# Retention attention and squared-ReLU FFN on one core: attention on 64-wide PE tiles, hand-fixed engine orders, weights by column slices

## Chip, cores, metric

One core of a Trainium2 chip. The metric is device time in microseconds (us) of that core, lower is better. Every ratio compares a kernel with the kernel before on the same chip in the same rounds. PE is the tensor engine, DVE the vector engine, ACT the scalar engine, POOL the GpSimd engine, SP the engine that issues the DMAs; SPq is SP's own queue of instructions, PEld are PE's weight loads, PSUM is the memory that PE writes to. In profile lines L288 is line 288 of the kernel, hp and op are the outputs of the FFN's first and second layer, tp a chunk's transposes, st its scores, yt its y, c the carry into the state. The span is the time from the first to the last instruction of the profiled execution.

## The reference, cut

```python
# q, k, v: (4, 8, 768, 64) float32; 8 heads, gamma[h] = 1 - 2**(-5-h)
for t in range(S):
    state = gamma * state + k[t] (x) v[t]          # (64 x 64) for each head
    y[t] = scale * q[t] @ state
# x = y as (3072 tokens, 512)
h = maximum(x @ w_in, 0)                           # w_in  (512, 2048)
out = (h * h) @ w_out                              # w_out (2048, 512), out (3072, 512)
```

The kernels work in chunks of 128 tokens, 24 in all, six to a sequence. In a chunk, scores k·q are masked and multiplied with v, and what earlier chunks left is added through a state. The FFN works on blocks of chunks: a first layer of 16 groups of 4 matmuls, then a second layer of 16 matmuls of 512 columns for each chunk.

## The kernel before

A scheduler orders the instructions. Parts (`...` marks cuts):

```python
# order of loads: chunks 0 to 3, all of w_in, all of w_out, then chunk 4 and on
if not w_in_issued and t + 2 == (chunks_per_blk[0] - 1):
    while w_in_q:  w_in_q.pop(0)()       # 4 rows of blocks, 1 MB each
    while w_out_q: w_out_q.pop(0)()      # 4 x 1 MB
...
def stage_b(m, s_prev):                  # y = v^T p + s^T q, 128 columns wide
    for hh in range(2):
        ytile = ps_yt.tile([P, 4, P], FP32, tag=f"yt{hh}")
        for p in range(4):
            nc.tensor.matmul(ytile[:, p, :], lhsT=vs[:, 2*p:2*p+2, :], rhs=pt[:, 2*p+hh, :], ...)
            if i > 0:
                nc.tensor.matmul(ytile[:, p, :], lhsT=s_prev[:, p, :], rhs=qT[:, p, :], ...)
        nc.scalar.activation(xt[rows, 0:4, off:off+C], ytile[rows, :, :], AF.Copy)   # half is used
    ...                                   # 4 matmuls for the carry, add, two memsets
...
def ffn_steps(tb):                        # blocks of 512 tokens
    for fb in range(NFB):
        ...                               # 4 matmuls of 512 columns, relu on ACT, square on DVE
        yield
    if tb == 0:
        cast_w_out()                      # after block 0's whole first layer
    for q4 in range(TB // 128):
        ...                               # 16 matmuls of 512 columns, copy, store
        yield
```

Of the kernel before, what the change touches and what calls it, by code (L numbers as in the profile page):

```python
# [18 lines left out]
def kernel(  # L20
# [14 lines left out]
    NTOK = B * S  # L35
    assert D == 64 and H == 8 and DM == H * D
    C = 128
    assert S % C == 0
    NCH = S // C
    if NTOK % 512 == 0:  # L40
        blk_sizes = [512] * (NTOK // 512)
    else:
        blk_sizes = [NTOK]
    assert sum(blk_sizes) == NTOK
    blk_starts = [int(sum(blk_sizes[:i])) for i in range(len(blk_sizes))]
    TBMAX = max(blk_sizes)
    NTB = len(blk_sizes)
    NFB = DFF // 128
    NCB = DM // 128
    assert NFB * 128 == DFF  # L50
    scale = 1.0 / float(np.sqrt(D))
    gammas = [1.0 - 2.0 ** (-5.0 - h) for h in range(H)]

    const = ctx.enter_context(tc.tile_pool(name="const", bufs=1))
    xtpool = ctx.enter_context(tc.tile_pool(name="xtpool", bufs=1))
    ldpool = ctx.enter_context(tc.tile_pool(name="ldpool", bufs=3))
    work = ctx.enter_context(tc.tile_pool(name="work", bufs=2))
    qkvpool = ctx.enter_context(tc.tile_pool(name="qkvpool", bufs=3))
    qktpool = ctx.enter_context(tc.tile_pool(name="qktpool", bufs=3))
    spool = ctx.enter_context(tc.tile_pool(name="spool", bufs=2))  # L60
    hpool = ctx.enter_context(tc.tile_pool(name="hpool", bufs=1))
    wstage = ctx.enter_context(tc.tile_pool(name="wstage", bufs=1))
    opool = ctx.enter_context(tc.tile_pool(name="opool", bufs=3))
    ps_tp = ctx.enter_context(tc.tile_pool(name="ps_tp", bufs=1, space=bass.MemoryType.PSUM))
    ps_st = ctx.enter_context(tc.tile_pool(name="ps_st", bufs=1, space=bass.MemoryType.PSUM))
    ps_yt = ctx.enter_context(tc.tile_pool(name="ps_yt", bufs=1, space=bass.MemoryType.PSUM))
    ps_c = ctx.enter_context(tc.tile_pool(name="ps_c", bufs=1, space=bass.MemoryType.PSUM))
    ps_f = ctx.enter_context(tc.tile_pool(name="ps_f", bufs=2, space=bass.MemoryType.PSUM))
# [11 lines left out]
    )  # L80
    cmask = const.tile([P, P], BF16)
# [10 lines left out]
    lng = const.tile([P, H], FP32)  # L92
    for h in range(H):
        nc.gpsimd.memset(lng[:, h : h + 1], float(np.log(gammas[h])))
    ex_i = const.tile([P, NCH, H], I32)
    nc.gpsimd.iota(
        ex_i[:], pattern=[[C, NCH], [0, H]], base=0, channel_multiplier=1
    )
# [8 lines left out]
    qf = const.tile([P, NCH, H], FP32)  # L107
    nc.scalar.activation(qf[:], ex_f[:], AF.Exp)
    nc.vector.tensor_scalar_mul(qf[:], qf[:], scale)
    kf = const.tile([P, NCH, H], FP32)  # L110
    nc.scalar.activation(kf[:], ex_f[:], AF.Exp, scale=-1.0)

    w_in_bf = const.tile([P, NCB, DFF], BF16)
    w_out_bf = const.tile([P, NFB, DM], BF16)
    w_in_f = wstage.tile([P, NCB, DFF], FP32)
    w_out_f = wstage.tile([P, NFB, DM], FP32)
    w_in_v = moe_w_in.rearrange("(cb p) f -> p cb f", p=P)
    w_out_v = moe_w_out.rearrange("(fb p) n -> p fb n", p=P)

    w_in_q = [  # L120
        (lambda cb=cb: nc.sync.dma_start(w_in_f[:, cb, :], w_in_v[:, cb, :]))  # L121
        for cb in range(NCB)
    ]
    w_out_q = []
    per = min(4, NFB)
    for fb0 in range(0, NFB, per):
        n = min(per, NFB - fb0)
        w_out_q.append(
            lambda fb0=fb0, n=n: nc.sync.dma_start(
                w_out_f[:, fb0 : fb0 + n, :], w_out_v[:, fb0 : fb0 + n, :]  # L130
            )
        )

    def flush_w_out():
        while w_out_q:
            w_out_q.pop(0)()

    def cast_w_in():
        for cb in range(NCB):
            if cb % 2 == 0:  # L140
                nc.vector.tensor_copy(w_in_bf[:, cb, :], w_in_f[:, cb, :])
            else:
                nc.scalar.activation(w_in_bf[:, cb, :], w_in_f[:, cb, :], AF.Copy)  # L143

    def cast_w_out():
        for fb in range(NFB):
            if fb % 2 == 0:
                nc.vector.tensor_copy(w_out_bf[:, fb, :], w_out_f[:, fb, :])
            else:
                nc.scalar.activation(w_out_bf[:, fb, :], w_out_f[:, fb, :], AF.Copy)  # L150

    xts = [
        xtpool.tile([P, NCB, blk_sizes[tb]], BF16, name=f"xt{tb}")
        for tb in range(NTB)
    ]

    def token_block(tok0):
        for tb in range(NTB):
            if blk_starts[tb] <= tok0 < blk_starts[tb] + blk_sizes[tb]:
                return tb  # L160
        raise ValueError(tok0)

    actx: dict = {}

    def stage_a0(m):
        b, i = chunk_batches[m]
        qn = ldpool.tile([P, H, D], FP32)
        nc.sync.dma_start(qn[:], q[b, :, i * C : (i + 1) * C, :].rearrange("h s d -> s h d"))
        kn = ldpool.tile([P, H, D], FP32)
        nc.sync.dma_start(kn[:], k[b, :, i * C : (i + 1) * C, :].rearrange("h s d -> s h d"))  # L170
        vn = ldpool.tile([P, H, D], FP32)
        nc.sync.dma_start(vn[:], v[b, :, i * C : (i + 1) * C, :].rearrange("h s d -> s h d"))

        qs = qkvpool.tile([P, H, D], BF16)
        nc.vector.tensor_tensor(  # L175
            out=qs[:],
            in0=qn[:],
            in1=qf[:, i, :, None].to_broadcast([P, H, D]),
            op=ALU.mult,
        )  # L180
        ks = qkvpool.tile([P, H, D], BF16)
        nc.vector.tensor_tensor(  # L182
            out=ks[:],
            in0=kn[:],
            in1=kf[:, i, :, None].to_broadcast([P, H, D]),
            op=ALU.mult,
        )
        vs = qkvpool.tile([P, H, D], BF16)
        nc.vector.tensor_copy(vs[:], vn[:])

        tp = ps_tp.tile([P, H, P], BF16)
        for p in range(4):
            nc.tensor.transpose(tp[:, p, :], qs[:, 2 * p : 2 * p + 2, :], ident[:])  # L193
        for p in range(4):
            nc.tensor.transpose(tp[:, 4 + p, :], ks[:, 2 * p : 2 * p + 2, :], ident[:])  # L195
        qkT = qktpool.tile([P, H, P], BF16)
        nc.scalar.activation(qkT[:], tp[:], AF.Copy)  # L197
        actx[m] = dict(qs=qs, ks=ks, vs=vs, qkT=qkT)

    def stage_a1(m):  # L200
        cm = actx[m]
        qkT = cm["qkT"]
        qT = qkT[:, 0:4, :]
        kT = qkT[:, 4:8, :]
        st_ps = ps_st.tile([P, 2, 4, P], FP32)
        for p in range(4):
            for hh in range(2):
                rows = slice(64 * hh, 64 * (hh + 1))
                nc.tensor.matmul(  # L209
                    st_ps[:, hh, p, :],  # L210
                    lhsT=kT[rows, p, :],
                    rhs=qT[rows, p, :],
                    start=True,
                    stop=True,
                )
        pt = work.tile([P, H, P], BF16)
        pt_v = pt.rearrange("s (p hh) t -> s hh p t", hh=2)
        nc.vector.tensor_tensor(  # L218
            out=pt_v,
            in0=st_ps[:],  # L220
            in1=cmask[:, None, None, :].to_broadcast([P, 2, 4, P]),
            op=ALU.mult,
        )
        cm["pt"] = pt

    def stage_b(m, s_prev):
        b, i = chunk_batches[m]
        cm = actx.pop(m)
        ks, vs, pt = cm["ks"], cm["vs"], cm["pt"]
        qT = cm["qkT"][:, 0:4, :]  # L230
        tok0 = b * S + i * C
        tb = token_block(tok0)
        off = tok0 - blk_starts[tb]
        xt = xts[tb]

        for hh in range(2):
            ytile = ps_yt.tile([P, 4, P], FP32, tag=f"yt{hh}")
            for p in range(4):
                h = 2 * p + hh
                nc.tensor.matmul(  # L240
                    ytile[:, p, :],
                    lhsT=vs[:, 2 * p : 2 * p + 2, :],
                    rhs=pt[:, h, :],
                    start=True,
                    stop=(i == 0),
                )
                if i > 0:
                    assert s_prev is not None
                    nc.tensor.matmul(  # L249
                        ytile[:, p, :],  # L250
                        lhsT=s_prev[:, p, :],
                        rhs=qT[:, p, :],
                        start=False,
                        stop=True,
                    )
# [5 lines left out]
        if i == NCH - 1:  # L261
            return None
# [68 lines left out]
    for t in range(-2, NCHUNK):  # L331
# [8 lines left out]
        if 0 <= t + 1 < NCHUNK:  # L340
            stage_a1(t + 1)
# [58 lines left out]
```

## Time and profile before

| | before |
|---|---|
| time | 246.35 us (2 runs, 246.2 to 246.5) |
| PE busy | 223.1 of 246.7 us, 90% |
| share of the chain that ended last | FFN matmuls hp 33% and op 32% |
| w_in in the chain | 15.2 us of DMA |

These are rows of the profile page of the kernel before: busy tenths in 40 equal slices (6.2 us each), the granted clock of PE in tenths, the busy tenths of the DMA engines, and GB/s.

```profile
PE   0395459999999999999999999999999999999994
...
PEclk9999558999999999999999999999999999999999
DMA  6999996998535999389698714100220001210022
GB/s 139 226 265 409 379 390 172 229 187 191 143 86 126 197 230 176 85 213 213 137 178 170 200 58 116 43 4 7 78 89 0 0 3 43 85 43 3 2 83 85
```

PE is dense from the seventh slice on. Nearly all that can be won without less work is in the first six. The first rows of GB/s also give two rates: q, k and v come in rows of 256 bytes at about 220 GB/s, the weights at 380 to 410.

The chain that ended last, from 15.9 us (columns: start, duration, what):

```profile
15.94 15.17 DMA w_in_f<-in_moe_w_in_dram
...
31.13 1.92 ACT w_in_bf L143
...
34.39 14.29 PE hp L288 x53
```

The first steady FFN matmul starts at 34.39 us, after the last part of w_in has landed and been cast.

PE in time in the steady part: start, duration from first start to last end, tile, shape, count. A duration holds the latency of the last matmul, so the cost of a group is the distance to the next start.

```profile
110.67 1.03 PE L288 MATMUL hp<-xt_135,w_in_bf 128*128 128x512 bf16 x4
111.53 0.39 PE L193 MATMUL tp<-ident,qs 128*128 128x128 bf16 x4
111.75 0.39 PE L195 MATMUL tp<-ident,ks 128*128 128x128 bf16 x4
112.07 0.40 PE L209 MATMUL st_ps<-qkT 64*128 64x128 bf16 x8
112.40 0.62 PE L240 MATMUL ytile<-pt,vs 128*128 128x128 bf16 x8
112.86 0.39 PE L265 MATMUL c_ps<-vs,ks 128*128 128x128 bf16 x4
113.08 4.67 PE L288 MATMUL hp<-xt_135,w_in_bf 128*128 128x512 bf16 x20
```

This chunk begins a sequence, so eight state matmuls are missing. Four full matmuls take 0.22 us (0.055 each). From the second transposes to the scores it is 0.32 us, 0.10 more: the change to 64-row tiles. Two lines of the chain mark a whole block (64 + 64 FFN matmuls and four chunks of attention), 35.37 us:

```profile
110.83 0.86 PE hp L288 x4
...
146.20 0.86 PE hp L288 x4
```

### The profile page before, as it was taken

To read this page: it belongs to the slowest core of one execution; us is meant where nothing else is said; L and a number is where in the kernel's file an instruction comes from. 1 tells how busy PE (TensorE), PEld (TensorE's weight loads), DVE (VectorE), ACT (ScalarE), POOL (GpSimd) and SP (SyncE) were. 2 spreads that over 40 slices of the span, in tenths; PEclk is the share of its full clock that TensorE was granted. 3 is DMA by queue.
4 is the path that set the end of the run, shared out by engine and by line. 5 is a ranking of instruction groups with operands and counts; after the bars stand their busy time and mean duration, and the time that the engine had idled before them with its cause. 6 is when DMAs were issued, how large, how long until landed. Compare 5 with 4: busy or idle time off the path is not lost.

```text
span 246.7 us, 3969 instructions
## 1 busy us (share of the span) xinstructions
PE 223.1 (90%) x1584; PEld 117.6 (48%) x1584; DVE 122.5 (50%) x225; ACT 129.8 (53%) x205; POOL 14.1 (6%) x57
## 2 busy tenths in 40 slices
PE   0395459999999999999999999999999999999994
PEld 0374013455555555445655455555465554444441
DVE  0797125775766888117888018674037630044200
ACT  2256376945637877118775137883158661176210
POOL 2001000000100010000000001000000000000000
PEclk9999558999999999999999999999999999999999
DMA  6999996998535999389698714100220001210022
GB/s 139 226 265 409 379 390 172 229 187 191 143 86 126 197 230 176 85 213 213 137 178 170 200 58 116 43 4 7 78 89 0 0 3 43 85 43 3 2 83 85
DMA packets 81042, 33.81 MB, mean 137 GB/s; under 512 B 75392, under 2 KB 75392, under 8 KB 80512
## 3 DMA queue, kind: packets, MB, share of 16 engines
q1 hardware_dynamic: 81024, 33.56, 55.0%
q8 instruction: 12, 0.20, 0.4%
q14 instruction: 6, 0.05, 0.1%
HBM read 27.26 MB, written 6.29 MB: 136 GB/s over the span
## 4 chain that ended last, share of the span: by engine, by line
PE 78%; DMA 8%; ACT 8%; SPq 2%; DVE 2%; issue 1%; ACTq 0%
PE hp L288 33%; PE op L304 32%; DMA w_in_f<-in_moe_w_in_dram 6%; ACT qkT L197 4%; PE ytile L240 3%; PE ytile L249 3%; PE st_ps L209 3%; DMA vn<-in_v_dram 2%; PE tp L193 2%; PE tp L195 2%; PE c_ps L265 1%; ACT xt_134 L257 1%; SPq L121 1%; ACT w_in_bf L143 1%; DVE qs L175 1%
## 5 line engine op out<-in xcount | busy, mean ns | idle before, releaser
L288 PEld LDWEIGHTS <-w_in_bf 128*128 128x128 bf16 x384 | 36.9, 99 | 51.9 <-issue 6.7
L312 ACT ACTIVATE osb<-op 128x512 f32<-128x512 f32 x24 | 14.3, 598 | 58.4 <-PE op L304 55.7
L218 DVE TENSOR_TENSOR pt<-st_ps,cmask 128x1024 bf16<-128x1024 f32 x24 | 29.3, 1220 | 5.4 <-PE st_ps L209 5.0
L197 ACT ACTIVATE qkT<-tp 128x1024 bf16<-128x1024 bf16 x24 | 24.5, 1021 | 12.3 <-PE tp L195 11.4
L175 DVE TENSOR_TENSOR qs<-qn,qf 128x512 bf16<-128x512 f32 x24 | 16.4, 686 | 21.2 <-PE tp L193 12.3
L240 PE MATMUL ytile<-pt,vs 128*128 128x128 bf16 x192 | 24.2, 224 | 1.6 <-DVE pt L218 1.3
L288 PE MATMUL hp<-xt_133,w_in_bf 128*128 128x512 bf16 x64 | 19.2, 446 | 6.0 <-ACT w_in_bf L143 4.1
L249 PE MATMUL ytile<-qkT,s_new 128*128 128x128 bf16 x160 | 21.1, 220 | 0.0
L240 PEld LDWEIGHTS <-vs 128*128 128x128 bf16 x192 | 17.6, 100 | 2.8 <-issue 0.4
L296 DVE TENSOR_TENSOR h_2576<-h_2576 128x512 bf16<-128x512 bf16 x16 | 6.8, 425 | 21.7 <-ACT h_2576 L295 21.7
L277 POOL MEMSET s_new<- 64x256 bf16 x20 | 6.5, 326 | 182.6 <-DVE s_new L276 132.7
L249 PEld LDWEIGHTS <-s_new 128*128 128x128 bf16 x160 | 15.7, 98 | 2.5 <-POOL s_new L278 1.3
L182 DVE TENSOR_TENSOR ks<-kn,kf 128x512 bf16<-128x512 f32 x24 | 16.4, 685 | 0.5 <-DMA kn<-in_k_dram 0.5
L265 PE MATMUL c_ps<-vs,ks 128*128 128x128 bf16 x80 | 8.4, 232 | 8.9 <-DVE ks L182 8.9
L296 DVE TENSOR_TENSOR h_2197<-h_2197 128x512 bf16<-128x512 bf16 x16 | 6.8, 424 | 19.4 <-ACT h_2197 L295 19.4
L304 PE MATMUL op<-w_out_bf,h_452 128*128 128x512 bf16 x64 | 16.3, 380 | 0.0
L288 PE MATMUL hp<-xt_134,w_in_bf 128*128 128x512 bf16 x64 | 15.8, 379 | 0.1
L288 PE MATMUL hp<-xt_136,w_in_bf 128*128 128x512 bf16 x64 | 14.6, 379 | 0.1
L288 PE MATMUL hp<-xt_135,w_in_bf 128*128 128x512 bf16 x64 | 14.6, 379 | 0.0
L288 PE MATMUL hp<-xt_137,w_in_bf 128*128 128x512 bf16 x64 | 14.5, 379 | 0.0
L288 PE MATMUL hp<-xt_138,w_in_bf 128*128 128x512 bf16 x64 | 14.0, 379 | 0.0
L304 PE MATMUL op<-w_out_bf,h_1332 128*128 128x512 bf16 x64 | 14.0, 379 | 0.0
(57 smaller groups left out, 310.5 us busy)
## 6 DMA issues: line engine op xcount, KB each, us to landing
qn<-in_q_dram SPq DMA_DIRECT2D x24, 256.0 KB, 4.8
kn<-in_k_dram SPq DMA_DIRECT2D x24, 256.0 KB, 4.4
vn<-in_v_dram SPq DMA_DIRECT2D x24, 256.0 KB, 4.7
out_dram<-osb SPq DMA_DIRECT2D x24, 256.0 KB, 2.1
w_in_f<-in_moe_w_in_dram SPq DMA_DIRECT2D x4, 1024.0 KB, 12.0
w_out_f<-in_moe_w_out_dram SPq DMA_DIRECT2D x4, 1024.0 KB, 17.8
```

The source lines that it names most:

```text
L175: nc.vector.tensor_tensor(out=qs[:], in0=qn[:], in1=qf[:, i, :, None].to_broadcast([P, H, D]), op=ALU.mult,)
L182: nc.vector.tensor_tensor(out=ks[:], in0=kn[:], in1=kf[:, i, :, None].to_broadcast([P, H, D]), op=ALU.mult,)
L197: nc.scalar.activation(qkT[:], tp[:], AF.Copy)
L209: nc.tensor.matmul(st_ps[:, hh, p, :], lhsT=kT[rows, p, :], rhs=qT[rows, p, :], start=True, stop=True,)
L218: nc.vector.tensor_tensor(out=pt_v, in0=st_ps[:], in1=cmask[:, None, None, :].to_broadcast([P, 2, 4, P]), op=ALU.mult,)
L240: nc.tensor.matmul(ytile[:, p, :], lhsT=vs[:, 2 * p : 2 * p + 2, :], rhs=pt[:, h, :], start=True, stop=(i == 0),)
L249: nc.tensor.matmul(ytile[:, p, :], lhsT=s_prev[:, p, :], rhs=qT[:, p, :], start=False, stop=True,)
L265: nc.tensor.matmul(c_ps[:, p, :], lhsT=ks[:, 2 * p : 2 * p + 2, :], rhs=vs[:, 2 * p : 2 * p + 2, :], start=True, stop=True,)
L288: nc.tensor.matmul(hp[:, :TB], lhsT=w_in_bf[:, cb, fb * 128 : (fb + 1) * 128], rhs=xt[:, cb, :], start=(cb == 0), stop=(cb == NCB - 1),)
L296: nc.vector.tensor_mul(h2[:, fb, :TB], h2[:, fb, :TB], h2[:, fb, :TB])
L304: nc.tensor.matmul(op[:], lhsT=h2[:, fb, q4 * 128 : (q4 + 1) * 128], rhs=w_out_bf[:, fb, :], start=(fb == 0), stop=(fb == NFB - 1),)
L312: nc.scalar.activation(osb[:], op[:], AF.Copy)
```

## The change

The intent: y and the carry on 64-wide tiles of PE, two at a time, in place of 128-wide matmuls of which half is thrown away; the state summed in PSUM over a sequence and the decay applied when y is read out, which takes copies and memsets away; the order of each engine's instructions fixed by hand; two first blocks of 256 tokens and w_in by column slices, so that the FFN can start when a quarter of w_in is there.

The diff, cut to its core:

```diff
+    blocks = [[0, 1], [2, 3]]                       # then blocks of 4 chunks
+    ctx.enter_context(tc.manual_schedule())
...
+    for m in range(4):
+        load_chunk(m)
+    for s in range(NSL):
+        load_w("i", s)                              # column slices of w_in, 1 MB each
...
-                nc.tensor.matmul(ytile[:, p, :], lhsT=vs[:, 2*p:2*p+2, :], rhs=pt[:, h, :], ...)
-                    nc.tensor.matmul(ytile[:, p, :], lhsT=s_prev[:, p, :], rhs=qT[:, p, :], ...)
+                    nc.tensor.matmul(yt[r, p, :], lhsT=s_bf[r, p, :], rhs=kqT[r, 1, p, :], ...)   # 64x64
+                nc.tensor.matmul(yt[r, p, :], lhsT=vs[:, 2*p+hh, :], rhs=pt[:, hh, p, :], ...)    # 128x64
+                    nc.tensor.matmul(c[r, p, :], lhsT=ks[:, h, :], rhs=vs[:, h, :], ...)          # 128x64
...
+    load_chunk(4)
+    load_w("o", 0)
+    load_chunk(5)
+    load_w("o", 1)
+    load_chunk(6)
+    load_w("o", 2)
+    load_chunk(7)
+    load_w("o", 3)
+    load_chunk(8)
...
+    q1 = all_f1(1)                                  # block 1's first layer, 16 groups
+    for x in range(NFB // 2):
+        q1[x]()
+        if x % 2 == 0:
+            cast_w("o", x // 2)                     # half on DVE, half on ACT
+    weave(q1[NFB // 2 :] + all_f2(0) + all_f2(1), stages(blocks[2]))
```

`stages` lists the attention steps of a block (for each chunk: scores of the chunk before, its three casts, its transposes, the output of the chunk two before), and `weave` spreads them between FFN steps. Casts of w_out stand in ACT's and DVE's fixed order, so the relu of block 1's eighth group stands behind the cast of the last slice.

## The prediction

> What bounds the kernel now. The engine table gives PE 223 of 246.7 us (90%). The chain of waits holds 65% in the FFN matmuls (hp, op); their 768 matmuls of 512 columns start 0.216 us apart (64 in 13.8 us), so 166 us of the span cannot go. From 45 us on the windows table shows PE busy almost without a gap. The loss is at the start: the first steady FFN matmul comes at 34.4 us, after w_in's casts, which wait for w_in's DMA (chain: 15.2 us); by then PE has done only 4 of 24 chunks of attention and 8 FFN matmuls, and the granted clock is 0.5 until about 38 us. The DMA slices show 256-byte q/k/v traffic saturating at about 220 GB/s (3.6 us a chunk) and weights at about 395 GB/s (2.65 us a MB).
>
> What the change does to PE in steady state. A middle chunk took about 2.0 us: 8 transposes 0.44, 8 scores 0.33, 16 y matmuls 0.9, 4 state matmuls 0.22. The 64-row scores start 28 ns apart, full ones 55 ns, so two tiles do run together; estimated from that, y falls to 16 x 28 ns = 0.45 and the state stays near 0.2. But the scores cost about 0.1 us of gap on each side in the timeline. The Trainium skill ("TensorEngine Tiling (Array Packing)", Key Properties) says changing the tiling mode drains the engine; the trace agrees (0.10 and 0.12 us). The new order has about five switches a chunk in place of two. It also says (Restrictions) that column tiling disables fast weight load; no run shows that yet. I estimate 1.75 us a chunk, so about 4 us saved over 20 chunks, not 10. Copies removed on ACT (1.2 us a chunk), POOL memsets and lighter DVE work are off the critical path.
>
> What it does to the start. Two blocks of 256 tokens and w_in column slices let FFN begin near 22 us instead of 25 to 34. But w_out's four slices are now queued behind chunks 4 to 7, and their casts stand in ACT's and DVE's order inside block 1's first FFN layer: the relu of its eighth group comes after the cast of the last slice. Bytes before that slice: 8.39 MB of weights and 6.29 MB of q/k/v. At the measured rates: 2.2 + 21.2 + 28.6 = 52 us, plus lag and cast, about 54 us. Until then PE can do only 4 chunks of attention, block 0's first layer and ten groups of block 1: a hole of some 20 us, mostly from 32 to 54. At 54 us the old kernel has done 89 FFN matmuls and 6 chunks; the new one 52 equivalents and 4.
>
> Sum: 54 + 716 x 0.216 (155) + 20 x 1.75 (35) + slow clock after the hole 2 + tail 3.6 + in-order stalls 3 to 5 (cast to turn on DVE: 1.5 us cast, 1.2 us mask) = about 253 us.
>
> Predicted 253 us, range 245 to 261. Faster by over 2%: 7%; within 2%: 35%; slower by over 2%: 58%.
>
> What would show it: last w_out slice landing at 50 to 56 us; PE tenths near 1 to 3 between 32 and 54 us, with waits ending in the w_out casts on ACT/DVE; steady FFN from about 55 us; a chunk's attention at 1.5 to 2.0 us of PE with gaps of 0.1 us at each mode switch; the y multiply off the chain; PE dense afterwards.
>
> What would make it wrong: DMA delivering the mix faster, so that the hole closes by 45 us; mode switches that cost nothing and pairs truly at 28 ns (attention 1.3 us, 8 us less); or column tiles loading weights serially at over 50 ns each (6 to 8 us more), or stalls in DVE's fixed order at every chunk.

## The result, and the profile after

| | before | after |
|---|---|---|
| time | 246.35 us | 260.36 us (2 runs, 259.56 and 261.15) |
| ratio, 95% interval | | 1.0585 (1.048 to 1.069) |
| PE busy | 223.1 us | 219.8 us |
| PE at work with no gap over 1 us from | 34 us | 60 us |

A ratio is the mean time of one kernel's fast runs over that of the other's of the same rounds, so it is not quite the ratio of the medians. Four more runs of the changed kernel later (after_again, below) gave 260.45 us and a ratio of 1.0619.

The same rows of the page, after (slices of 6.5 us):

```profile
PE   1546674207899999999999999999999999999994
...
PEclk9999998555999999999999999999999999999999
DMA  7999889981011398021992124971119601210022
GB/s 175 246 316 397 218 213 271 278 246 33 0 43 54 97 261 200 0 82 43 217 246 64 40 77 114 247 175 39 44 47 252 149 0 43 81 43 0 0 81 81
```

PE works more than before in slices one, two and four to six, and then there is a hole: 4, 2, 0 in the slices from 39 to 58 us, in which the clock falls to a half. The DMA rate in slices five to nine is 213 to 278 GB/s, though weights are among the bytes.

The chain that ended last, through the hole:

```profile
38.75 4.21 SPq L81
...
43.08 0.78 SPq L92
...
45.25 4.13 SPq L81
...
49.49 7.71 DMA wo_368<-in_moe_w_out_dram
...
57.23 1.06 ACT w_out_bf_176 L166
58.28 0.28 ACT h_1_563 L299
...
58.59 0.29 DVE h_1_563 L300
58.88 0.61 DVE ks_628 L179
...
59.54 1.05 PE tp_641 L194 x8
```

The last slice of w_out lands at 57.2 us, is cast, then a relu, a square and a cast of chunk 4 follow in the fixed orders, and PE goes on at 59.54 us. On the way the chain runs through SP's own queue: loads that took over 4 us only to be issued. Here is that queue, with each load's start and the time its issue took:

```profile
30.42 5.59 SPq L81 DMA_DIRECT2D vn_350<-in_v_dram  x1
36.12 0.78 SPq L92 DMA_DIRECT2D wo_352<-in_moe_w_out_dram  x1
36.94 0.51 SPq L81 DMA_DIRECT2D kn_354<-in_k_dram  x1
37.49 1.21 SPq L81 DMA_DIRECT2D qn_356<-in_q_dram  x1
38.75 4.21 SPq L81 DMA_DIRECT2D vn_358<-in_v_dram  x1
43.08 0.78 SPq L92 DMA_DIRECT2D wo_360<-in_moe_w_out_dram  x1
```

A slice, k and q go out at once, and v is held. The list of DMA issues gives 6.9 us from issue to landing for the slice issued at 36.12, so it landed at 43.02; the issue of v ended at 38.75 + 4.21 = 42.96. The other slices do the same to 0.1 us: v's issue ended at 36.01, 49.38 and 57.14, and the slice before it landed at 36.08, 49.48 and 57.19. It is not a free buffer that v waits for: the pool has five, and the four v's held here take those of chunks 0 to 3, whose casts had ended by 22.3 us.

The steady part, PE in time for a full chunk's output:

```profile
110.98 1.03 PE L311 MATMUL op_1248<-w_out_bf_175,h_2_1002 128*128 128x512 bf16 x4
111.94 0.41 PE L235 MATMUL yt_1272<-kqT_1089,s_1202 64*64 64x128 bf16 x8
112.28 0.41 PE L246 MATMUL yt_1272<-pt_1114,vs_1062 128*64 128x128 bf16 x8
112.52 0.29 PE L262 MATMUL c_912<-vs_1062,ks_1060 128*64 128x64 bf16 x8
112.75 1.04 PE L311 MATMUL op_1248<-w_out_bf_176,h_2_1002 128*128 128x512 bf16 x4
```

The 24 tiled matmuls cost 112.75 - 111.94 = 0.81 us, and 0.10 us of gap ahead of them (110.98 + 4 x 0.216 = 111.84). The 20 wide ones of before cost 20 x 0.055 = 1.1 us. So the tiles save 0.2 us a chunk. But in another place PE waits (start and distance again):

```profile
128.73 1.03 PE L292 MATMUL hp_6_1505<-xt_1175,w_in_bf_170 128*128 128x512 bf16 x4
129.78 0.40 PE L194 MATMUL tp_1512<-ident,ks_1492 128*128 128x128 bf16 x4
130.12 0.40 PE L194 MATMUL tp_1512<-ident,qs_1493 128*128 128x128 bf16 x4
```

From 128.73 four matmuls last to 129.59; the transposes start 0.19 us later, and their second half 0.34 instead of 0.22 us after the first. They wait for DVE's casts. A block's distance in the chain is as good as that of before, 35.31 us:

```profile
87.52 0.86 PE hp_0_1003 L292 x4
...
122.83 0.86 PE hp_0_1435 L292 x4
```

With as much FFN work and eight chunks of attention behind it, the kernel is at 87.5 us where the one before, with a little more of the next attention done, began its second block at 73.3. So, on these profiles, all of the loss is in the start.

### The profile page after: what moved, and what is told of

It is laid out like the page before. It is cut to its first block, busy times and chain, and to the rows that moved or that the text cites. A ratio compares the mean times of both kernels' runs of the same rounds, so it can differ in the third digit from the quotient of the medians.

```text
span 259.4 us, 4217 instructions
## 1 busy us (share of the span) xinstructions
PE 219.8 (85%) x1728; PEld 112.4 (43%) x1728; DVE 122.9 (47%) x244; ACT 116.6 (45%) x198; POOL 3.0 (1%) x26
## 3 DMA queue, kind: packets, MB, share of 16 engines
HBM read 27.26 MB, written 6.29 MB: 129 GB/s over the span
## 4 chain that ended last, share of the span: by engine, by line
PE 77%; SPq 9%; DMA 6%; ACT 3%; DVE 2%; issue 1%; ACTq 0%
SPq L81 9%; DMA wi_120<-in_moe_w_in_dram 3%; DMA wo_368<-in_moe_w_out_dram 3%; PE op_2593 L311 1%; PE op_1307 L311 1%; PE op_2164 L311 1%; PE op_1732 L311 1%; PE op_924 L311 1%; PE op_854 L311 1%; PE op_817 L311 1%; PE op_1673 L311 1%; PE op_1366 L311 1%; PE op_1211 L311 1%; PE op_2652 L311 1%; PE op_2534 L311 1%; PE op_2497 L311 1%
## 5 line engine op out<-in xcount | busy, mean ns | idle before, releaser
L292 PEld LDWEIGHTS <-w_in_bf_171 128*128 128x128 bf16 x112 | 11.1, 104 | 16.6 <-issue 5.1
L292 PEld LDWEIGHTS <-w_in_bf_170 128*128 128x128 bf16 x112 | 10.9, 100 | 14.4 <-issue 3.9
L292 PEld LDWEIGHTS <-w_in_bf_169 128*128 128x128 bf16 x112 | 10.9, 103 | 8.8
L292 PEld LDWEIGHTS <-w_in_bf_172 128*128 128x128 bf16 x112 | 10.4, 99 | 9.9 <-DVE w_in_bf_172 L165 1.7
L300 DVE TENSOR_TENSOR h_6_2690<-h_6_2690 128x512 bf16<-128x512 bf16 x16 | 6.8, 425 | 10.1 <-ACT h_6_2690 L299 10.1
L300 DVE TENSOR_TENSOR h_5_2288<-h_5_2288 128x512 bf16<-128x512 bf16 x16 | 6.6, 422 | 7.8 <-ACT h_5_2288 L299 7.8
L300 DVE TENSOR_TENSOR h_2_1002<-h_2_1002 128x512 bf16<-128x512 bf16 x16 | 6.6, 422 | 7.8 <-ACT h_2_1002 L299 7.8
L300 DVE TENSOR_TENSOR h_4_1869<-h_4_1869 128x512 bf16<-128x512 bf16 x16 | 6.6, 422 | 7.8 <-ACT h_4_1869 L299 7.8
L300 DVE TENSOR_TENSOR h_3_1434<-h_3_1434 128x512 bf16<-128x512 bf16 x16 | 6.6, 422 | 7.3 <-ACT h_3_1434 L299 7.3
L311 PEld LDWEIGHTS <-h_6_2690 128*128 128x128 bf16 x64 | 6.3, 98 | 7.5
L311 PEld LDWEIGHTS <-h_4_1869 128*128 128x128 bf16 x64 | 5.8, 98 | 6.5
L311 PEld LDWEIGHTS <-h_2_1002 128*128 128x128 bf16 x64 | 5.8, 98 | 6.5
L311 PEld LDWEIGHTS <-h_5_2288 128*128 128x128 bf16 x64 | 5.8, 98 | 6.5
L311 PEld LDWEIGHTS <-h_3_1434 128*128 128x128 bf16 x64 | 5.8, 98 | 6.5
L300 DVE TENSOR_TENSOR h_0_376<-h_0_376 128x256 bf16<-128x256 bf16 x16 | 4.7, 292 | 5.9 <-ACT h_0_376 L299 4.6
L300 DVE TENSOR_TENSOR h_1_563<-h_1_563 128x256 bf16<-128x256 bf16 x16 | 4.6, 290 | 6.1 <-ACT h_1_563 L299 5.9
L194 PE MATMUL tp_641<-ident,ks_628 128*128 128x128 bf16 x4 | 0.6, 305 | 7.6 <-DVE ks_628 L179 7.6
L194 PE MATMUL tp_183<-ident,ks_177 128*128 128x128 bf16 x4 | 0.6, 305 | 5.3 <-DVE ks_177 L179 5.3
L194 PE MATMUL tp_327<-ident,ks_310 128*128 128x128 bf16 x4 | 0.6, 308 | 5.3 <-DVE ks_310 L179 5.3
L292 PE MATMUL hp_8_634<-xt_391,w_in_bf_171 128*128 128x256 bf16 x4 | 1.0, 406 | 4.6 <-ACT h_1_563 L299 4.6
L155 ACT ACTIVATE yf<-t_f,lnp 128x128 f32<-128x128 f32 (+1 forms) x8 | 4.2, 603 | 0.0
L311 PEld LDWEIGHTS <-h_1_563 128*128 128x128 bf16 x32 | 2.8, 98 | 3.1
```

What stands on the lines that cost most here:

```text
L155: nc.scalar.activation(yf[:, p, lo:hi], t_f[:, lo:hi], AF.Exp, scale=lnp[:, p : p + 1])
L194: nc.tensor.transpose(tp[:, j, p, :], src[:, 2 * p : 2 * p + 2, :], ident[:])
L292: nc.tensor.matmul(hp[:, :n], lhsT=w_in_bf[s][:, cb, r * P : (r + 1) * P], rhs=xts[b][:, cb, :n], start=(cb == 0), stop=(cb == NCB - 1),)
L300: nc.vector.tensor_mul(h2[:, fb, :n], h2[:, fb, :n], h2[:, fb, :n])
L311: nc.tensor.matmul(op[:], lhsT=h2s[b][:, fb, j * P : (j + 1) * P], rhs=w_out_bf[part][:, r, :], start=(fb == 0), stop=(fb == NFB - 1),)
```

## The experiments

Theory A: the hole is the wait for w_out's last slice, which comes late because chunks 5 to 7 stand before it and because slices and chunks in turn starve the DMA queue (A2), and because the fixed orders have nothing else to do meanwhile. Theory B, the rival: the time goes in the steady part, to mode switches of PE and waits between engines. Eleven runs were made, one of them the changed kernel again; the names with "v" are attempts at a better kernel. They were run at other times.

### e1_wout_first: w_out before chunks 5 to 8

```diff
     load_chunk(4)
     load_w("o", 0)
-    load_chunk(5)
     load_w("o", 1)
-    load_chunk(6)
     load_w("o", 2)
-    load_chunk(7)
     load_w("o", 3)
+    load_chunk(5)
+    load_chunk(6)
+    load_chunk(7)
     load_chunk(8)
```

> The changed kernel with the loads in another order: chunk 4, the four w_out slices, then chunks 5 to 8. Theory A (the hole before 59.5 us is the wait for the last w_out slice, which lands at 57.2 us because chunks 5 to 7 stand before it): the last slice lands at 41 to 44 us, the hole ends near 45 us, and the time falls by 12 to 15 us to 245 to 249 us. Theory B (the time went in the steady part, through mode switches and fixed orders): the landing moves but the total changes by under 3 us.

Measured: 248.14 us, ratio to before 1.0105 (1.005 to 1.016). The cast of the last slice starts at 44.2 us, having waited for its DMA; 12.2 us are gone by moving three lines, and PE goes on at 46.5 us in place of 59.5:

```profile
44.21 1.06 ACT L166 ACTIVATE w_out_bf<-wo 128x1024 bf16<-128x1024 f32 x1 [0.88 <-DMA wo<-in_moe_w_out_dram]
```

The bracket gives the idle time before and what ended it. Theory A holds, B does not: nothing in the steady part was touched.

### e2_grouped: the same bytes, not in turn

```diff
     load_chunk(4)
-    load_w("o", 0)
     load_chunk(5)
-    load_w("o", 1)
     load_chunk(6)
-    load_w("o", 2)
     load_chunk(7)
+    load_w("o", 0)
+    load_w("o", 1)
+    load_w("o", 2)
     load_w("o", 3)
     load_chunk(8)
```

> Same bytes before the last w_out slice as in the changed kernel, but chunks 4 to 7 together and then the four slices, not one of each in turn. Theory A2 (my 52 us for the landing was too small because taking turns starves the queue: the third load of each chunk is issued only when the weight slice before it has landed): the last slice lands at 52 to 54 us, the DMA share has no dips under 0.7 between 20 and 52 us, and the time falls by 3 to 5 us to 255 to 257 us. Rival (small and large packets in one stretch cost the DMA engines more, or every kernel runs below the rates I used): landing stays at 56 to 58 us and the time within 1 us of 260.

Measured: 258.08 us (257.16 to 258.26), ratio 1.0497 (1.047 to 1.053). The last slice's cast starts at 53.23 us, as expected, where in four profiles of the order in turn (the changed kernel twice, e4_wide, e6_cast_early) it starts at 57.2, 54.9, 57.7 and 56.7 us. The time fell by 2.3 us, less than the 3 to 5 expected, though the profiled span fell by 4: the landing of the order in turn varies by nearly 3 us from run to run, and the first profile had caught a late one. A dip of the DMA share was also still there between 27 and 35 us (0.88), after w_in's slices. Busy time by stretch (start:end, length, then PE, weight loads, DVE, ACT, POOL, and last the PE clock, the DMA share and GB/s), first the changed kernel, then e2_grouped:

```profile
35.00:43.00 8.00, 4.70 (x40) 3.91 (x41) 3.54 (x11) 4.48 (x10) 0.00 (x0) 1.00 0.90 245
43.00:52.00 9.00, 2.87 (x12) 1.53 (x11) 2.52 (x6) 3.20 (x6) 0.00 (x0) 0.53 0.97 250
```

```profile
35.00:43.00 8.00, 3.67 (x32) 3.14 (x33) 2.35 (x7) 2.88 (x7) 0.00 (x0) 1.00 1.06 267
43.00:53.20 10.20, 4.74 (x20) 2.67 (x19) 3.78 (x9) 4.81 (x9) 0.00 (x0) 0.51 1.06 369
```

Grouped, the share stays at 1.06 and the slices come at 369 GB/s. Two later runs fit: e5_casts_late, in turn, landed at 56.6 us, and e7_as_summed, grouped, at 53.5. So loading in turn costs 1.4 to 4.4 us of landing here.

### e3_two_queues: w_out on ACT's queue

```diff
-            nc.sync.dma_start(t[:], w_out_v[...])
+            nc.scalar.dma_start(t[:], w_out_v[...])
...
         nc.scalar.activation(dst[:, 2:4, :], src[:, 2:4, :], AF.Copy)     # end of cast_w
+        if which == "i":
+            load_w("o", s)
...                                        # and no load_w("o", s) between the chunks
```

> w_out's slices on ACT's DMA queue, each issued after the cast that frees its buffer; chunks 4 to 8 stay on SP's queue. Theory A2: no slice stands before a chunk's load any more, so the dips of the DMA share under 0.7 between 27 and 52 us go, the last slice lands at 45 to 52 us, and the time falls by 5 to 12 us. Rival (packets of two sizes share the engines badly whatever the queue): the mean rate between 27 and 52 us stays near 240 GB/s and the last slice lands no earlier than 54 us.

Measured: 248.07 and 248.84 us, 252.48 and 253.9 over 1.5% above that and so counted as slow (ratio of the fast ones 1.0103). The cast of the last slice starts at 44.81 us, just under the expected 45 to 52, and there is no dip (the lowest share of one microsecond from 27 to 43 us is 0.93):

```profile
27.00:35.00 8.00, 4.94 (x64) 3.57 (x58) 5.62 (x14) 5.78 (x13) 0.00 (x0) 1.00 1.13 335
35.00:43.00 8.00, 5.46 (x46) 4.45 (x47) 4.58 (x14) 5.85 (x13) 0.00 (x0) 1.00 1.08 334
```

Packets of 256 bytes and 2 KB together move at 335 GB/s when neither stands before the other in a queue; the rival, that the mix itself is slow, falls. The slices also got a larger part of the bytes here (3.7 of 5.35 MB from 27 to 43 us, where the changed kernel moved 4.2 of 7.5 MB from 27 to 57.2), so the gain is not all A2's. Against the two rates of the kernel before, 395 and 220 GB/s, which would give these mixes 318 and 295 GB/s, the two queues ran 5% above the sum and the one queue 16% below it. Why one queue holds v until the slice has landed (how much it can hold, counted how) no run shows.

### e4_wide: 128-wide attention

```diff
-                        yt[r, p, :],
-                        lhsT=s_bf[r, p, :],
-                        rhs=kqT[r, 1, p, :],
+                        yt[:, p, :],
+                        lhsT=s_bf[:, 2 * hh : 2 * hh + 2, :],
+                        rhs=kqT[:, 1, p, :],
...                                        # likewise 8 y matmuls and 4 for the carry
```

> Wrong on purpose: the y, state and carry matmuls are issued 128 columns wide as in the kernel before (16 of 128x128 and 4 of 128x128 a chunk in place of 24 on 64-wide tiles), all else as in the changed kernel. Theory C (pairs on 64-wide tiles do start at 28 ns each, but the extra mode switches give back half: net 0.2 us a chunk): a block of 4 chunks takes 0.8 us longer than the 35.3 us of the changed kernel, and the time rises by 3 to 5 us. Rival (tiles save nothing, or cost): within 1 us, or faster.

Measured: 263.56 us, ratio 1.0727 (1.069 to 1.076), wrong values as intended. A block of four chunks took 36.0 us in place of 35.3. So the tiles do save: 0.18 us a chunk, 3 to 4 us in all (the time rose by 3.1). They were not what made the kernel slower.

### after_again: the changed kernel once more

> The changed kernel itself once more, so that it has as many runs as its variants: 259 to 262 us, the last w_out slice landing at 56 to 58 us as before.

Measured: 260.45 us (258.89 to 262.05). Its profiled run was the fastest of the four; the cast of the last slice starts at 54.95 us there, a little under the expected landing.

### e5_casts_late: the same loads, another order of work

```diff
-    for x in range(NFB // 2):
+    for x in range(NFB):
         q1[x]()
-        if x % 2 == 0:
-            cast_w("o", x // 2)
-    weave(q1[NFB // 2 :] + all_f2(0) + all_f2(1), stages(blocks[2]))
+        if x % 8 == 7:
+            cast_w("o", x // 8)
+    for x, f in enumerate(stages(blocks[2])):
+        f()
+        if x == 7:
+            cast_w("o", 2)
+    cast_w("o", 3)
+    for f in all_f2(0) + all_f2(1):
+        f()
```

> Loads exactly as in the changed kernel; only the places of w_out's casts and of the second layer in the fixed orders change: block 1's first layer and the attention of chunks 4 to 7 come before the cast of the last slice. Theory A says that the hole has two parents, the late landing and an order that has nothing else to do: the last slice lands at 57 us as before, but PE has by then done 7 more groups of block 1 (3 us) and four chunks of attention (7.5 us), so the time falls by 8 to 11 us to 249 to 252 us. If the hole were DMA alone, and the order without part in it: within 2 us of the changed kernel.

Measured: 256.15 us, 4.3 us less, half of what was expected. The order does have a part in the hole, but I had costed four chunks of attention at 7.5 us of PE. Alone they took from 47.4 to 67.3 us:

```profile
47.35 0.40 PE L194 MATMUL tp<-ident,ks 128*128 128x128 bf16 x4 [2.01 <-DVE ks L179]
...
49.20 0.40 PE L206 MATMUL st<-kqT 64*128 64x128 bf16 x8 [1.11 <-ACT kqT L196]
51.51 0.61 PE L194 MATMUL tp<-ident,ks 128*128 128x128 bf16 x4 [1.92 <-DVE ks L179]
...
67.32 15.38 PE L311 MATMUL op<-w_out_bf,h 128*128 128x512 bf16 x64
```

The brackets give the idle time before and its releaser. Each chunk waits 1.9 to 2.0 us for DVE, which does a mask and three casts a chunk, and the first two also 1.1 us for ACT's copy: 5 us a chunk, with a mean granted clock of 0.57. Here attention was cheap only between FFN matmuls. The slice landed at 56.6 us; from then on PE no longer waited for it.

### e6_cast_early: a chunk's casts before the mask

```diff
+            if n < len(ms):
+                seq.append(lambda m=ms[n]: a_cast(m))
             if 0 <= n - 1 < len(ms):
                 seq.append(lambda m=ms[n - 1]: a_score(m))
             if n < len(ms):
-                seq.append(lambda m=ms[n]: a_cast(m))
                 seq.append(lambda m=ms[n]: a_turn(m))
```

> In the woven part a chunk's three casts are put before the mask multiply of the chunk before, not after it. Theory D (in 12 of 16 steady chunks PE waits 0.19 us at the transposes for the cast on DVE, the tiles' saving goes there): the gap before the transposes falls from 0.40 to 0.22 us and the time by 2 us, 1.5 to 3. Rival (the gap is a fixed cost of turning to the transposes): no change.

Measured: 256.89 us (255.51 to 258.53), 3.5 us less. The gap before the transposes is 0.216 us, one FFN matmul, in all 16 steady chunks; in the changed kernel it was 0.40 in 8 of them (not in 12, as I had counted). The mean distance of blocks fell from 35.18 to 34.56 us. The last FFN matmuls and the transposes after them:

```profile
124.16 1.90 PE L292 MATMUL hp<-xt,w_in_bf 128*128 128x512 bf16 x8
125.90 0.39 PE L194 MATMUL tp<-ident,ks 128*128 128x128 bf16 x4
```

Eight matmuls from 124.16 are done at 125.89, and the transposes start at once. The wait was DVE's order, not a cost of transposing. It explains 2.5 us in the steady part; as much went in the first weaving, where PE took 25.4 in place of 28.0 us from chunk 4's transposes to block 2. That makes 5 us where the medians differ by 3.5: the profiled run had its slice land at 56.7 us, 1.7 later than after_again, whose span is 3.3 us longer, so these two close.

### v1_start: chunks 0 and 1, w_in, chunks 2 and 3, w_out

```diff
-    for m in range(4):
+    for m in range(2):
         load_chunk(m)
     for s in range(NSL):
         load_w("i", s)
+    for m in range(2, 4):
+        load_chunk(m)
...
+        q0[fb]()                          # block 0's whole first layer, casts before each quarter
+    a_cast(2)                             # then chunks 2 and 3 alone
...
+    for f in q2[:3]:                      # block 1's first layer with w_out's casts, then
+        f()
+    weave(q2[3:], stages(blocks[2]))
```

> A version meant to beat both: chunks 0 and 1, then w_in's slices, then chunks 2 and 3, then w_out's slices, then the rest; block 0's first layer before chunks 2 and 3; w_out's casts after each quarter of block 1's first layer; three steps of the second layer before the weaving. Theory A: last w_out slice lands at 37 to 42 us, PE dense from 30 to 35 us on, time 231 to 238 us. If mode switches and fixed orders were the main loss, it would stay above 246.

Measured: 248.82 us, far above the expected 231 to 238. The first FFN matmul did start at 15.7 us, but the 16 matmuls of each of the first two quarters started 0.22 us apart, half speed, with 1.4 us of waiting for a cast before a quarter; and chunks 2 and 3, alone as in e5_casts_late, took from 34.4 to 42.5 us. PE was dense from 42.5, not from 30 to 35 us. The last slice landed at 40.6 us, inside the expected 37 to 42, but PE was not what waited for it; what I had left out was the chain of copies.

### e7_as_summed: e2_grouped and e6_cast_early together

> Both terms of my sum set as I had taken them: chunks 4 to 7 together before the slices (landing at 53 us measured, I had said 54) and the casts before the mask (no wait at the transposes). If the miss of 7 us is those two terms and nothing else, the time is 253 to 256 us, about 5 to 6 us under the changed kernel's 260.4. If something else is in it, it stays above 257 us.

Measured: 252.41 us (251.47 to 253.44), ratio 1.0293 (1.025 to 1.034): 8 us under the changed kernel, a little more than the 5 to 6 expected. That it lies within 1 us of the predicted 253 is luck: the 253 had 3 to 5 us of stalls in it, which this kernel has not, and took PE to go on at 54 us, where it went on at 55.8 here. The corrected sum does close: from 55.8 us to the end of the span it was 195.5 us, the terms 155, 35, 2 and 3.6 give 195.6 without stalls, and with the 1.8 us between span and time (below) that is 253.2, against 253.14 of the profiled run. Each alone gave 2.3 and 3.5 us; the landing's jitter, nearly 3 us in the order in turn, is in those differences.

### v2_filled: loads of e1, casts of e6, and FFN work beside every attention step

```diff
+    early = {1: lambda: a_cast(4), 4: lambda: a_turn(4), 8: lambda: a_score(4)}
+    casts = {5: 0, 9: 1, 12: 2, 15: 3}
-    for x in range(NFB // 2):
+    for x in range(NFB):
         q1[x]()
-        if x % 2 == 0:
-            cast_w("o", x // 2)
-    weave(q1[NFB // 2 :] + all_f2(0) + all_f2(1), stages(blocks[2]))
+        if x in early:
+            early[x]()
+        if x in casts:
+            cast_w("o", casts[x])
+    q2 = all_f2(0) + all_f2(1)
+    rest = stages(blocks[2])
+    del rest[3], rest[0:2]                # chunk 4's cast, transposes, scores are done
+    q2[0]()
+    weave(q2[1:], rest)
```

> Loads: chunk 4, w_out's slices, chunks 5 to 8. Block 1's first layer runs through, with chunk 4's cast, transposes and scores and w_out's casts in between; the casts before the mask; FFN work between all later attention steps. Last slice lands at 43 to 45 us; at that time block 1's first layer is done, so the time is 236 to 241 us, faster than both kernels. Above 244 us the order is still at fault somewhere.

Measured: 238.18 us (238.04 to 239.43), correct, ratio to before 0.9727 (0.968 to 0.977): faster than both kernels. The last slice landed at 43.3 us, as expected; block 1's first layer was then not done, as I had said, but ran until 46.3. The list of waits has no wait of ACT or DVE for w_out left. Its page:

```profile
PE   0464859899999999999999999999999999999993
...
PEclk9999999999999999999999999999999999999999
```

No slice under 8 tenths from 35.5 us on but the last, and no half clock in the row.

### v3_early_weights: v2 with w_in before chunks 2 and 3

```diff
-    for m in range(4):
+    for m in range(2):
         load_chunk(m)
     for s in range(NSL):
         load_w("i", s)
+    for m in range(2, 4):
+        load_chunk(m)
...                                        # chunks 2 and 3 between groups 9 to 15 of block 0
```

> As v2_filled, but w_in's slices are loaded before chunks 2 and 3, whose attention is put between block 0's later groups. First FFN matmul near 16 us in place of 22. If the filled order keeps PE busy the time is 2 to 5 us under v2_filled; if PE at half clock and the chain of copies in chunks 2 and 3 take it back, as in v1_start, it is equal or worse.

Measured: 244.24 us, 6 us slower than v2_filled: the second of the outcomes named. FFN starts at 15.5 us, but 16 matmuls take 3.6 us, and block 1's first layer begins at 41.5 us, where in v2_filled half of it is done (37 to 46 us). Here an earlier start was worth nothing: it was slow work with waits between.

## Why the prediction was wrong in size

The direction and the mechanism were right: slower, by a hole at the start that ends with the cast of w_out's last slice, while the tiles save little. The size was off: 6.7 us more were forecast, 14 measured. Point by point:

- **"8.39 MB of weights and 6.29 MB of q/k/v ... 2.2 + 21.2 + 28.6 = 52 us, plus lag and cast, about 54 us." This is the step that failed.** The last slice landed at 57.2 us in the first profile (54.9 to 57.7 in five of this order), and PE went on at 59.5. Lag and cast were 2.3 us, as allowed; the landing was the mis-sized term. I had added bytes at rates taken from stretches in which one kind of load had the queue. In turn on one queue, each chunk's third load was held until the slice before it had landed, and the mean rate from 27 to 57.2 us was 247 GB/s in place of the 295 that the two rates of the kernel before give for a slice and a chunk (1.83 MB in 6.2 us). e2_grouped, the same bytes in another order, landed at 53.2; e3_two_queues had no dips.
- **"about 253 us" was a sum of pieces of the trace, that is a span, and was put down as a time.** In all twelve profiled runs after the prediction, the time of the run is 1.7 to 1.9 us above its span (261.15 against 259.4). That is 1.8 us of the miss. For the kernel before, the page says 246.7 and the times 246.2 to 246.5; the time of the profiled execution is not among them, so the trap could not be seen there.
- **The rest of the sum held.** From 59.5 us to the end of the span it was 199.9 us; the terms 155, 35, 2, 3.6 and 3 to 5 give 199.6 with the stalls at 4. So the first profile closes: 253.6 + 5.5 + 0.3 + 1.8 = 261.2, against 261.15 measured.
- **"I estimate 1.75 us a chunk" was right for the work:** without the waits (e6_cast_early) a chunk takes (34.56 - 128 x 0.2158) / 4 = 1.73 us. "In-order stalls 3 to 5 (cast to turn on DVE)" was right too, at its upper end: about 2.5 us in the steady part and 2.5 in the first weaving. Together they mean that the steady part gained nothing, which the block distances of 35.4 and 35.3 us say as well.
- **Mode switches.** The Trainium skill ("TensorEngine Tiling (Array Packing)", Key Properties) has it that a change of tiling mode drains the engine. The trace fits, and each of the five switches a chunk costs the same 0.10 us. Going in, the first score starts 0.312 us after an FFN matmul that takes 0.216. Coming out, the next matmul starts 0.148 us after the last score, where two pairs of scores lie 0.052 apart (the 0.12 of the prediction comes out if 0.028 is set against it). From the state's 64x64 tiles to y's 128x64 tiles the distance is 0.146, again in place of 0.052.
- **Column tiling and weight loads.** The same page (Restrictions) says that it disables fast weight load; I gave 6 to 8 us to that as a risk. It cost nothing that the trace shows: the two of a pair started 3 ns apart and the next pair 52 ns after (28 ns a matmul on average), matmuls and loads alike.
- **"PE tenths near 1 to 3 between 32 and 54 us."** The hole was from 39 to 59 us. Block 0 ended at 37.9, because its quarters waited for casts of w_in (1.1 to 1.4 us each) and its first matmuls ran at half speed (256 columns in 0.215 us at 22.6 us, in 0.109 from 28.6 us on).
- **"FFN begin near 22 us"** was right (22.55), and so was that it would not help.

What stays open: why SP's queue holds a load until the slice before it has landed (a limit of what one queue takes in would fit, but no run varied it), and why the landing varies by almost 3 us between runs.

## What to carry to other kernels

When loads of two kinds stand in turn in one queue, do not trust a sum of bytes over their separate rates (52 us here, where 54.9 to 57.7 were measured): look in the issuing engine's own queue for issues that are held, and put what a fixed order needs first in front. In hand-fixed orders, let no instruction of a busy engine wait for a late load while work that needs nothing of it stands behind; and place a chain of small copies only beside matmuls that can hide it, since alone it took 5 us a chunk where woven it took 1.7. A start made earlier is worth only what PE does in it, as v3_early_weights showed.

## What the Trainium skill lacked or had wrong

- "DMA: Bandwidth & Descriptors" (Queues, rings and completion order) tells of SP's and ACT's own rows of rings and that the engines take turns between rows; e3_two_queues fits that (335 GB/s from both queues together), though no trace here shows the turns themselves. No page gives how much such a queue takes in before an issue is held, or says that the hold can last until an earlier, larger DMA of the queue has landed: 4.1 to 5.6 us, after all four slices of w_out.
- The same page (Specifications) gives a limit of about 358 GB/s from HBM for one core. Only further down does it say that this is the share with both cores of a pair streaming, and that a core alone gets more. This program runs on one core: from 20 to 27 us the changed kernel moved 384 GB/s on average, with 414 in one microsecond, all of it reads from HBM.
- "TensorEngine Tiling (Array Packing)" (Key Properties) says that a mode change drains, not what it costs: 0.10 us for each change at full clock here. That transposes among full matmuls cost no such gap (0.216 us from an FFN matmul to the transposes, 0.056 back) it does not say either.
- "TensorE: Matmul & The Clock Gate" (Part 1: The HAM clock gate) says that PE starts throttled until it has been busy for some microseconds, and warns that the recorded clock events can be unreliable. The runs fit both, so this is no fault of the page, but a reader of the profile's clock row would be misled: at 22.6 us matmuls of 256 columns started 0.215 us apart while the row reads full clock; from 28.6 us on they started 0.109 apart.
